# One-core attention and MoE kernel: attention visits split in two, a longer list of warm-up matmuls, unit 0's last rows by quadrants, and a new instruction order

## Chip, cores and metric

The kernel runs on one core of one Trainium2 chip. The metric is the device time in microseconds of one execution, the median of several runs. One further execution was taken under the hardware profiler, and all rows below come from it.

## What is computed (reference, cut)

A linear attention with per-channel decay (batch 4, 8 heads, 768 tokens, head size 48) gives a 3072 x 384 matrix; a two-layer MLP (384 to 2048 to 384) with a piecewise quadratic gate follows.

```python
for t in range(S):                       # per batch and head; state is 48 x 48
    cur = einsum('bhd,bhe->bhde', u * kt, vt)
    y[:, :, t] = einsum('bhd,bhde->bhe', rt, state + cur)
    state = wt[..., None] * state + einsum('bhd,bhe->bhde', kt, vt)
x = y.transpose(0, 2, 1, 3).reshape(3072, 384)
h = x @ w_in
g = h where h >= 1, 0 where h <= -1, else (h + 1)**2 / 4
out = g @ w_out
```

## The kernel before

**Tiling.** The tokens are cut into 12 attention *units* of 256 tokens (u0 to u11), two to a *block* of 512 tokens (b0 to b5). The MLP runs block by block in *steps* over the 16 slices f of 128 hidden columns. The first 8 steps of each half of block 0 and the first 11 of each half of block 1 treat 256 tokens (half steps), the others 512 (whole steps); there are 115 steps, n0 to n114. Step n has on TensorE an IN (`product_in`, L1040, nine passes; for n0 to n7 `product_in_whole`, L1046, six passes in full fp32) and an OUT (`product_out`, L1070; for n0 to n7 `product_out_whole`, L1052). Between them ScalarE and VectorE form the gate (`g`, `gh`, `gl`, L819 to L825). An fp32 matmul appears in the trace as two passes, each with its own weight load.

**Attention on TensorE.** A unit visits TensorE several times between the products, with small matmuls (64 or 48 rows and columns) that occupy one quadrant of the array each. In order: AMONGu (`among` with u, units 0 to 3 only, 64 passes, L475), AMONG (`among` with k, 64 passes, L475), KTRANS (transposes of k, units 0 to 3, 4 passes per half, L515; from unit 4 on VectorE and small DMAs do this), UMAT (`umat`, 64 passes, L533), then CROSS and ALONG or, for late units, CORNERS, ALONG, CORNERS (all through `put`, L612, 128 passes). VectorE works between them: two scans per half unit (L434, L429), the products k*=y (L455) and r*=p (L505), masked copies out of PSUM (`picked`, L481), and the state chain (`chain`, L581 to L587) between UMAT and CROSS. r*=p overwrites what AMONGu reads, so it follows AMONGu on VectorE. AMONG needs both r*=p.

**Units 4 to 11 before.** `VISIT` gives each the step after which its attention is entered; `late` is true, and `first_visit` runs AMONG and UMAT as one TensorE operation, with a bank of the hidden product (`hp`) as fourth PSUM bank.

**Start.** `warm` (L311 to L312) writes zeros into all eight PSUM banks with one fp32 matmul of 128 x 128 x 512 each, 16 passes in all; it is first on TensorE, and AMONGu of unit 0 follows it. Unit 0 ends with SPREAD (`spread`, L718): its last rows are moved between the other rows with three 128 x 128 matmuls per group g, two groups, 12 passes; they are copied out before that (last_f, L723). x_all is then copied (L693) and IN n0 may start. LESS (`less`, L709) subtracts the high part of unit 0's x.

**Weights.** A weight slice is loaded by SP (`fetch`, L332, 768 KB), joined from two halves on VectorE (`join`, L336) and split into a high part on ScalarE (L358) and a low part by a subtraction on VectorE (L361).

**Order.** Every engine executes its own instructions in order. That order is `ORDER`, a list of operation numbers written out by hand; an operation's number is its place among the calls of `op()`. The costs in the `op()` calls order nothing while `ORDER` is given; they only place the zero matmuls that fill long gaps.

Of the kernel before, what the change touches and what calls it, by code (L numbers as in the profile page):

```python
# [28 lines left out]
HP = 64  # L29
# [6 lines left out]
NB = NT // WIDE  # L36
# [15 lines left out]
class Plan:  # L52
# [101 lines left out]
VISIT = {4: 37, 5: 46, 6: 56, 7: 63, 8: 71, 9: 78, 10: 87, 11: 94}  # L154
# [72 lines left out]
)  # L227


def attention_moe(tc, a):  # L230
# [149 lines left out]
    def attention(u, when, spare=None):  # L380
# [220 lines left out]
        if late:  # L601
            by.append(take())
# [538 lines left out]
```

## Time and profile before

| | us |
|---|---|
| median of 3 runs | 498.87 (498.66 to 499.46) |
| profiled execution | 497.06 |
| its span, first to last instruction | 495.2 |
| TensorE busy in the span | 485.5 (98%) |
| VectorE busy | 343.8 (69%) |
| ScalarE busy | 289.6 (58%) |
| GpSimd busy | 56.7 (11%) |

TensorE's busy time counts passes from start to modelled end, and passes overlap, so the rate of a stretch is better read from the distance between starts. VectorE's share is an average over a dense first quarter and a light rest.

### The profile page before, as it was taken

How to read it: one execution, taken by the hardware profiler on the slowest of the kernel's cores; microseconds unless marked ns; L12 is line 12 of the kernel's file. 1: busy time of each engine (PE TensorE's matmuls, PEld its weight loads, DVE VectorE, ACT ScalarE, POOL GpSimd, SP SyncE). 2: the span in 40 equal slices, each digit the busy share in tenths (PEclk: the TensorE clock that was granted, in tenths of full speed). 3: DMA queues.
4: the chain of work that ended last, by engine and by line, in shares of the span. 5: the costliest groups of instructions: out<-in, count | busy, mean ns of one | idle time of the engine just before them, and what ended most of it. 6: DMA issues, size and time to landing. Idle time of an engine off the chain costs nothing.

```text
span 495.2 us, 12991 instructions
## 1 busy us (share of the span) xinstructions
PE 485.5 (98%) x5402; PEld 404.8 (82%) x5402; DVE 343.8 (69%) x597; ACT 289.6 (58%) x592; POOL 56.7 (11%) x60
## 2 busy tenths in 40 slices
PE   9799999999999999999999999999999999999997
PEld 4688998778999988888888888888888888888886
DVE  6899999998758768659679679469556745332333
ACT  3799889866656536746736646346626625552551
POOL 2332121300110101110110330020001000000000
PEclk9899999999999999999999999999999999999999
DMA  8995736225544344345245454225221110200001
GB/s 316 406 374 169 256 115 217 88 60 158 166 111 149 66 133 159 103 113 161 38 131 175 108 139 150 48 79 154 43 66 44 29 33 16 66 1 1 1 0 66
DMA packets 58749, 58.29 MB, mean 118 GB/s; under 512 B 38016, under 2 KB 47424, under 8 KB 58688
## 3 DMA queue, kind: packets, MB, share of 16 engines
q1 hardware_dynamic: 58256, 56.78, 37.4%
q8 instruction: 43, 0.70, 0.6%
q10 hardware_dynamic: 432, 0.66, 0.4%
q14 instruction: 18, 0.15, 0.1%
HBM read 46.34 MB, written 4.72 MB: 103 GB/s over the span
## 4 chain that ended last, share of the span: by engine, by line
PE 89%; DVE 5%; ACT 2%; issue 2%; DMA 1%; POOL 0%; DVEq 0%; SPq 0%; POOLq 0%
PE h L1040 37%; PE acc L1070 36%; PE bank L612 4%; PE bank L475 2%; PE bank L533 2%; PE acc L1052 2%; PE bank L1070 1%; PE h L1046 1%; PE bank L312 1%; DMA rk<-in_rk 1%; DVE r L481 1%; DVE wt L361 1%; PE acc L612 1%; DVE gl L825 1%; DVE rk L505 1%
## 5 line engine op out<-in xcount | busy, mean ns | idle before, releaser
L1040 PE MATMUL h<-x,wt 128*128 128x512 f32 (+1 forms) x963 | 207.4, 365 | 0.5 <-DVE g L821 0.4
L1040 PEld LDWEIGHTS h<-x,wt 128*128 128x128 f32 x963 | 162.5, 188 | 32.0 <-DVE g L821 0.9
L1070 PE MATMUL acc<-gh,wt 128*128 128x512 f32 (+1 forms) x642 | 146.4, 359 | 0.0
L821 DVE SCALAR_TENSOR_TENSOR g<-g,h 128x512 f32<-128x512 f32 (+1 forms) x115 | 67.8, 593 | 95.6 <-ACT g L820 95.1
L819 ACT ACTIVATE g<-h 128x512 f32<-128x512 f32 (+1 forms) x115 | 60.4, 526 | 119.2 <-PE h L1040 117.4
L1070 PEld LDWEIGHTS acc<-gh,wt 128*128 128x128 f32 x642 | 107.9, 188 | 18.7
L825 DVE TENSOR_TENSOR gl<-g,gh 128x512 fp32r<-128x512 f32 (+1 forms) x107 | 68.9, 648 | 17.1 <-ACT gh L824 10.6
L1070 PE MATMUL acc<-gl,wt 128*128 128x512 f32 (+1 forms) x321 | 80.7, 358 | 0.0
L824 ACT CAST gh<-g 128x512 fp32r<-128x512 f32 (+1 forms) x107 | 59.1, 556 | 33.1 <-DVE g L821 22.3
L820 ACT ACTIVATE g<-g 128x512 f32<-128x512 f32 (+1 forms) x115 | 64.4, 561 | 3.1
L1070 PEld LDWEIGHTS acc<-gl,wt 128*128 128x128 f32 x321 | 55.2, 188 | 9.1
L434 DVE TENSOR_TENSOR_SCAN p<-wq,seeds 128x514 f32<-128x514 f32 x24 | 30.8, 1283 | 10.8 <-DMA kt<-p 7.2
L501 POOL TENSOR_TENSOR r<-cst,d 128x512 f32<-128x512 f32 x16 | 17.0, 1084 | 152.2 <-DVE d L498 71.8
L429 DVE TENSOR_TENSOR_SCAN y<-wq,seeds 128x514 f32<-128x514 f32 x24 | 30.1, 1254 | 0.8
L346 POOL CAST rr<-fl 128x768 f16<-128x768 f32 x16 | 21.3, 1332 | 71.2 <-ACT fl L342 32.7
L493 POOL TENSOR_TENSOR nk<-nk 128x768 f32<-128x768 f32 x8 | 15.3, 1913 | 96.8 <-DMA nk<-in_nk 87.9
L455 DVE TENSOR_TENSOR rk<-rk,y 128x512 f32<-128x512 f32 x24 | 17.1, 712 | 2.6 <-DMA rk<-in_rk 2.1
L505 DVE TENSOR_TENSOR rk<-rk,p 128x512 f32<-128x512 f32 x24 | 17.0, 717 | 0.7 <-DMA rk<-in_rk 0.4
L345 ACT ACTIVATE rr<-wraw 128x768 uint16<-128x768 uint32 x16 | 17.3, 1079 | 0.2 <-DVE wa L336 0.2
L342 ACT ACTIVATE fl<-wraw 128x768 f32<-128x768 f32 x16 | 14.7, 917 | 1.0 <-DVE wt L361 1.0
L481 DVE COPY_PREDICATED r<-cst,bank 128x512 f32<-128x512 int32 x20 | 14.5, 729 | 1.0 <-PE h L475 0.5
L612 PEld LDWEIGHTS bank<-rk,st 48*48 48x48 f32 x656 | 11.4, 119 | 4.2 <-issue 1.8
(116 smaller groups left out, 447.8 us busy)
## 6 DMA issues: line engine op xcount, KB each, us to landing
rk<-in_rk SPq DMA_DIRECT2D x24, 512.0 KB, 5.3
wraw<-in_wbits SPq DMA_DIRECT2D x16, 768.0 KB, 6.9
wq<-in_w SPq DMA_DIRECT2D x24, 258.5 KB, 3.0
nk<-in_nk SPq DMA_DIRECT2D x8, 768.0 KB, 4.9
vn<-in_v SPq DMA_DIRECT2D x11, 384.0 KB, 4.4
kt<-p SPq DMA_DIRECT2D x128, 32.0 KB, 1.9
fl<-in_w SPq DMA_DIRECT2D x12, 257.0 KB, 3.4
x<-last SPq DMA_DIRECT2D x66, 32.0 KB, 2.0
```

The costliest lines, as they stand in the source:

```text
L346: op("POOL", SIGN, due, [("fl", k)], ["rr_high"], lambda: G.tensor_copy(rr.bitcast(F16).rearrange("p (c two) -> p c two", two=2)[:, :, 1], s))
L429: V.tensor_tensor_scan(out=y_[:, ::-1], data0=w[:, SEG:0:-1], data1=sv[:, ::-1], initial=0.0, op0=ALU.mult, op1=ALU.add)
L434: V.tensor_tensor_scan(out=pv[:, q].rearrange("p n c -> p (n c)"), data0=w[:, 0:SEG], data1=sv, initial=0.0, op0=ALU.mult, op1=ALU.add,)
L505: op("DVE", 0.69, due, [("p", q)], [("r", slot[q])], lambda q=q: V.tensor_tensor(out=parts(q, 0), in0=parts(q, 0), in1=pv[:, q, :, 0:UT], ...
L612: PE.matmul(out=bank[by[g]][HP * half : HP * half + wide, lo : lo + C], start=first, stop=False, skip_group_check=True, **kw)
L819: op("ACT", c, due, [("b", 6 + hk)], [("g", gk)], lambda: nc.scalar.activation(gs, hs, AF.Relu, scale=0.5, bias=0.5))
L820: op("ACT", c, due, (), [("g", gk)], lambda: nc.scalar.activation(gs, gs, AF.Square))
L821: op("DVE", 0.13 + 0.53 * k, due, [("b", 6 + hk)], [("g", gk)], lambda: nc.vector.scalar_tensor_tensor(out=gs, in0=gs, scalar=1.0, in1=hs, ...
L824: op("ACT", c, due, [("g", gk)], [("gh", gk)], lambda: nc.scalar.copy(ghs, gs))
L825: op("DVE", 0.15 + 0.5 * k, due, [("g", gk), ("gh", gk)], [("gl", gk)], lambda: nc.vector.tensor_tensor(out=gls, in0=gs, in1=ghs.bitcast(F ...
L1040: nc.tensor.matmul(hp, lhsT=wx[f][:, cs], rhs=xt[:, j, :], start=n == 0, stop=n == 8)
L1070: nc.tensor.matmul(o, lhsT=wx[f][:, 384 + j * 128 : 512 + j * 128], rhs=gt[:, 0 : cs.stop - cs.start] if gt.shape[1] < cs.stop else gt[:, cs],
```

## The change

Five edits:

1. `VISIT` is empty. Units 4 to 11 are entered with their block (at its predecessor's first step), so `late` is false and AMONG and UMAT are two operations again, on the three rotating PSUM banks. The form CORNERS, ALONG, CORNERS is kept for them by the new `side`.
2. `warm` begins with 39 fp32 matmuls of 64 x 64 x 64 (78 passes) in one quadrant; the first three banks are then cleared by two matmuls each in diagonal quadrants (12 passes), the other five as before (10 passes).
3. `spread` uses two 64 x 64 matmuls in diagonal quadrants for each 128 x 128 one (24 passes), as a quadrant operation.
4. The cost of `first_visit` in the list is changed; with no late unit it is not used.
5. `ORDER` is new (1791 numbers for 1783). In it, among much else, unit 0's loads stand in the order w1, perm, rk1, w0, rk0, cst, v (before: w1, w0, perm, rk1, rk0, v, cst), three weight loads stand ahead of unit 1's loads (before: between them), IN n0 stands ahead of LESS, and between the two visits that were one there are two to nine products.

```diff
-VISIT = {4: 37, 5: 46, 6: 56, 7: 63, 8: 71, 9: 78, 10: 87, 11: 94}
+VISIT = {}
+SMALL = 39
+SIDE = 4
...
     def warm():
-        for b in bank:
+        for _ in range(SMALL):
+            PE.matmul(bank[0][0:64, 0:64], lhsT=zero[0:64, 0:64], rhs=zero[0:64, 0:64], start=True, stop=True)
+        for b in bank[0:3]:
+            for i in (slice(0, 64), slice(64, 128)):
+                PE.matmul(b[i], lhsT=zero[i, 0:64], rhs=zero[i].unsqueeze(1).broadcast_to([64, 4, 128]), start=True, stop=True)
+        for b in bank[3:8]:
             PE.matmul(b, lhsT=zero, rhs=zero.unsqueeze(1).broadcast_to([128, 4, 128]), start=True, stop=True)
...
-        late = spare is not None
+        late, side = spare is not None, u >= SIDE
...
-            op("PE", 1.64, due, [("k", slot[0]), ("k", slot[1]), *both, *turns, *vk], [("b", i) for i in (*ba, *bu)], first_visit, apart=True)
+            op("PE", 1.89, due, [("k", slot[0]), ("k", slot[1]), *both, *turns, *vk], [("b", i) for i in (*ba, *bu)], first_visit, apart=True)
...
         by = [take(), take()]
-        if late:
+        if side:
             by.append(take())
...
-                PE.matmul(yv[:, j], lhsT=perm[:, 128 * j : 128 * j + 128], start=False, stop=True, skip_group_check=True,
-                          rhs=last_f.rearrange("p (c g t) -> p c g t", c=2, g=2)[:, :, g, :])
+                for h in range(2):
+                    i, lo = slice(HP * h, HP * h + HP), 128 * j + HP * h
+                    PE.matmul(yv[i, j], lhsT=perm[i, lo : lo + HP], start=False, stop=True, skip_group_check=True,
+                              rhs=last_f.rearrange("p (c g t) -> p c g t", c=2, g=2)[i, :, g, :])
...
-                op("PE", 0.35, due, [("last_f", g), "perm", "nk", ("g", 2)], [("b", by[g])], lambda g=g: spread(g), fresh=False)
+                op("PE", 0.3, due, [("last_f", g), "perm", "nk", ("g", 2)], [("b", by[g])], lambda g=g: spread(g), fresh=False, apart=True)
...
-        if n == WHOLE:
-            for u in (2, 3):
-                attention(u, step_of(u))
+        if n == WHOLE or b and f == 0 and cs.start == 0 and b + 1 < NB:
+            for u in (2 * b + 2, 2 * b + 3):
+                if u not in VISIT:
+                    attention(u, step_of(u))
```

## Rows read from the trace of the kernel before

**Rows 1.** Stretches of 5 us: us, busy time of each engine, clock, DMA.
```profile
15.00:20.00 5.00, 2.74 (x112) 2.50 (x112) 4.18 (x8) 2.56 (x3) 1.21 (x2) 0.92 1.03 398
20.00:25.00 5.00, 4.56 (x29) 3.90 (x24) 4.22 (x8) 3.77 (x8) 2.06 (x1) 0.74 1.01 406
...
95.00:100.00 5.00, 4.47 (x20) 3.25 (x19) 5.00 (x5) 3.58 (x6) 3.44 (x2) 1.00 0.06 21
```

**Rows 2.** Timeline of the start: start us, us, engine, line, operation, [idle before <-releaser].
```profile
1.07 5.05 PE L312 MATMUL bank<-zero 128*128 128x512 f32 x6 [1.07 <-POOL zero L296]
...
2.94 0.34 PEld L312 LDWEIGHTS bank<-zero 128*128 128x128 f32 x1 [0.52 <-issue]
...
3.80 0.34 PEld L312 LDWEIGHTS bank<-zero 128*128 128x128 f32 x1 [0.52 <-issue]
...
5.96 2.74 PE L312 MATMUL acc<-zero 128*128 128x512 f32 x6
...
8.53 1.88 PE L312 MATMUL h<-zero 128*128 128x512 f32 x4
...
8.67 0.91 ACT L445 ACTIVATE nk<-rk,wq 128x256 f32<-128x256 f32 x2 [0.55 <-DMA rk<-in_rk]
...
10.34 1.02 PEld L475 LDWEIGHTS acc<-rk,nk 64*64 64x64 f32 x64 [0.76 <-ACT nk L445]
...
11.11 1.29 DVE L505 TENSOR_TENSOR rk<-rk,p 128x512 f32<-128x512 f32 x2 [0.22 <-PE acc L475]
11.43 0.85 PEld L515 LDWEIGHTS bank<-cst,rk 128*128 128x128 f32 x8
11.44 1.09 PE L515 MATMUL bank<-cst,rk 128*128 128x128 f32 x8
```

**Rows 3.** Stretches of 0.5 us around unit 0's ALONG, columns as in rows 1.
```profile
18.50:19.00 0.50, 0.50 (x44) 0.50 (x41) 0.47 (x3) 0.00 (x0) 0.00 (x0) 1.00 1.06 394
...
19.50:20.00 0.50, 0.50 (x26) 0.50 (x20) 0.00 (x0) 0.00 (x0) 0.00 (x0) 0.50 1.07 421
```

**Rows 4.** Chain that ended last, in order of time: start us, us, what.
```profile
16.06 1.44 issue
...
133.37 1.07 PE h L1040 x9
...
151.80 1.94 PE bank L612 x128
...
200.57 4.20 PE h L1040 x18
...
366.10 1.26 PE bank L533 x63
```

**Rows 5.** TensorE's costliest groups, one of them: busy us, mean ns, idle before.
```profile
L718 PE MATMUL acc<-g,nk 128*128 128x128 f32 x12 | 2.5, 391 | 0.3 <-ACT g L723 0.3
```

**Rows 6.** Timeline of TensorE around unit 2's AMONG and UMAT.
```profile
57.97 1.16 PE L475 MATMUL bank<-rk 64*64 64x64 f32 x64
59.06 1.33 PE L1040 MATMUL h<-x,wt 128*128 128x256 f32 x9
60.23 0.60 PE L515 MATMUL bank<-cst,rk 128*128 128x128 f32 x4
...
65.02 0.94 PE L533 MATMUL bank<-vn,kt 64*48 64x48 f32 x64
65.89 1.33 PE L1040 MATMUL h<-x,wt 128*128 128x256 f32 x9
```

**Rows 7.** Timeline of TensorE, one of the eight merged visits.
```profile
286.85 0.27 PE L475 MATMUL bank<-rk 64*64 64x64 f32 x1
...
287.83 1.12 PE L533 MATMUL bank<-vn,kt 64*48 64x48 f32 x64
288.88 1.66 PE L1070 MATMUL acc<-gh,wt 128*128 128x512 f32 x6
```

**Rows 8.** Timeline of TensorE around unit 3's first transposes.
```profile
99.95 0.66 PE L515 MATMUL bank<-cst,rk 128*128 128x128 f32 x4 [0.53 <-DVE r L481]
```

More of the change, by code (lines that the diff above doesn't have):

```diff
@@ L635, in along @@
         def along(heads=(0, 1)):
-            if not late and 0 in heads:
+            if not side and 0 in heads:
                 crossed(0)
@@ L656, in attention @@
         y512 = y_[:, 0:512].rearrange("p (a c t) -> p a c t", a=4, t=C)
-        if late:
+        if side:
             third_bank = bank[by[2]].rearrange("p (a c t) -> p a c t", a=4, t=C)
```

122 rows, old and new, of the table ORDER are left out of this document.

## The prediction, as put on record before the result was known

> **What bounds the kernel now.** I read the chain that ended last first, then TensorE's timeline, then the 5 us stretches. On the chain a whole product is 4.20/2 = 2.10 us for nine passes and a half product 1.07 us [rows 4]; the products stand on it back to back almost from the first to the last. So a microsecond by which TensorE's first product comes later is a microsecond at the end, unless TensorE waits somewhere later and the lateness is used up in that wait. There is such a wait, and VectorE makes it. VectorE is busy 5.00 of 5.00 us in 95 to 100, while TensorE has 4.47 [rows 1], and unit 3's transposes wait 0.53 us for a masked copy [rows 8].
>
> How much TensorE waits in all I take from a stretch without other shapes: unit 2's UMAT starts at 65.02 [rows 6], unit 4's CORNERS at 151.80 [rows 4], 86.78 us. Between them stand 16 whole products (33.6), 36 half ones (38.4) and the visits: two UMAT and two AMONG-like visits at about 1.05 and 1.28 with their turns [rows 6], four half transposes at 0.5 [rows 2], two CROSS with ALONG at 2.3 (the 1.94 of the 128 passes in rows 4, and its drain), one merged visit at 2.3. That is 84.5 us, so **2.3 us are waits for VectorE**.
>
> Before the first product the chain is one of dependencies: warm-up, AMONGu, r*=p, AMONG, UMAT, state chain, CROSS, ALONG, SPREAD, x_all, IN n0. VectorE idles there for lack of inputs: 0.82 us in 15 to 20 and 0.78 us in 20 to 25, 1.6 us in all [rows 1]. Two things are behind it. TensorE stands for 1.44 us in CROSS with nothing to wait for that the profile shows [rows 4], and the granted clock falls from 1.00 to 0.50 in the second half of ALONG [rows 3], after TensorE was busy for only 2.74 of 5 us [rows 1]. SPREAD then runs at 391 ns a pass [rows 5].
>
> **The change part by part.** *Warm-up.* A pass of 512 columns starts 0.86 us after the one before at the low level of the clock (1.2 GHz; loads at 2.94 and 3.80) and 0.43 us after it at the high one (2.4 GHz; six passes from 5.96 to 8.53) [rows 2]; the rate of the passes shows the level here. It changes near 5.5 us. Sixteen passes end at 5.96 + 10 x 0.43 = 10.25, and AMONGu starts at 10.34 [rows 2]. Its data were there earlier: the last scaled copy ends at 8.67 + 0.91 = 9.58 [rows 2]. So the warm-up sets the start, and any lengthening counts in full. A tiny pass has 64 columns, an eighth: 0.107 us low, 0.054 high. From 1.07 to 5.5 that is 41 passes, the other 37 take 2.0, up to 7.5. Twelve diagonal passes go two abreast: 6 x 0.43 = 2.6, or 3.0 if the pairs overlap only in part as they are ordered. Ten full passes take 4.3. The sum ends at 14.4 to 14.8, against 10.25: **+4.4 us** for AMONGu. Behind it wait r*=p (11.11 before, at once after AMONGu [rows 2]) and with it all of VectorE's queue, which has nothing to do between about 11 and 15 us, and ScalarE's copies of the transposes.
>
> The lower bound of this term comes from the nearest rows at the other end. In sets of four quadrants 44 passes touch half a microsecond at the high level and 26 at the low one [rows 3], 0.011 and 0.019 us each. If a lone tiny pass cost only its share of a set, 78 would take 0.9 to 1.5 us, more of the later passes would run at the low level, and the warm-up would end near 10.8: +0.5. I take 0.107, because one quadrant streams its own 64 columns whatever the other three do. The upper bound: if tiny passes in a quarter of the array don't raise the clock, they last 78 x 0.107 = 8.3 us to 9.4, some full passes follow at 0.86, and the end is near 17.5: +7.3.
>
> *What the start gives back.* With AMONGu 4.4 us late VectorE has a full queue, and its 1.6 us of idleness go but for 0.1: **-1.5**. The 1.44 us and the half-speed clock are inside this term. TensorE is denser there, so I expect the clock to stay up until ALONG; it may fall while TensorE waits for x_all at about 24 to 27 us, which would slow the first products: **+0.3** taken, 0 to 1.3 as bounds.
>
> *SPREAD.* 24 passes, two abreast, stream as long as 12; only the turn between quadrant and full passes moves behind it: 0. It is covered by VectorE, which in the new order has a scan ahead of last_f and another ahead of x_all; without that cover it saves some 0.1.
>
> *New order at the start.* Decoding the lists by counting operations: up to the state chain of unit 1 VectorE has 37 instructions instead of 38 (one weight subtraction less, about 0.97 us by the r*=p row scaled from 512 to 768 columns, 1.29/2 x 1.5 [rows 2]); TensorE has one product of the full kind less ahead of unit 1's CROSS (six passes of 256 columns, 6 x 0.21 = 1.3). Both engines are about as tight there as before: **+0.3**.
>
> *New order later.* At OUT n16 the same TensorE work stands ahead in both lists, but 99 VectorE instructions instead of 102; missing are a scan, a k*=y and two subtractions, and one weight join has come in, 2 us and more. At unit 3's CROSS TensorE has two more half products ahead and VectorE about the same. So VectorE's lead grows by 2 us or more where TensorE now waits, and the **-2.3** of waits go. Bounds: 0 and -2.3; there is no more to take.
>
> *Visits apart.* The merged visit takes 288.88 - 286.85 = 2.03 us [rows 7], and some are longer: one has 1.26 us in its UMAT on the chain [rows 4]; the eight average 2.13. Alone, AMONG takes 1.09 and UMAT 0.87 [rows 6], 1.96 together, and a second turn costs 0.1 ahead and 0.1 after (1.17 for the half product after AMONG [rows 6], against 1.07 [rows 4]). 2.16 against 2.03 to 2.13, for eight units: **+0.1**, 0 to +1.0. SP's and POOL's queues keep their instructions; only their order changes, and the unit loads keep the slack of a whole block.
>
> *A rule against the change.* The two transposes of unit 0 use all rows of the array in each pass, and eight loads and eight passes took 1.09 us together [rows 2]: loads and passes overlap although they share rows, and 0.107 stands. The Trainium skill says otherwise (TensorE: Matmul & The Clock Gate, Part 3: Packing small matmuls): a weight load overlaps running matmuls only when its row group is another one, and all tiny passes share theirs. The trace disagrees; by that rule the sum would be that of rival D, by the rows it is the one below.
>
> *Loads.* On SP's queue w0 of unit 0 now has perm and rk1 (704 KB) ahead of it, 1.8 us at about 400 GB/s [rows 1]; unit 1's first loads have two weights more ahead, 1.57 MB or 3.9 us. Both are hidden by the later AMONGu: 0. Without that cover the first would cost up to 1.8 us.
>
> Sum: 4.4 - 1.5 + 0.3 + 0.3 - 2.3 + 0.1 = **+1.3 us**. The profiled execution took 497.06 (span 495.2 and 1.9 around it), which makes 498.4. The median of the three runs lies 1.8 above the profiled one; I carry the difference over: 498.87 + 1.3 = 500.2.
>
> **Rivals.** *A: a tiny pass is cheap, and the kernel gets faster.* The place is the first 15 us. With the lower bound (+0.5) the sum is -2.6: 496.3. With the high-level price of 0.054 from the first pass on the warm-up ends near 12.4, the term is 2.2 and the sum -0.9: 498.0. It decides below 0.054 us a tiny pass. For it: no row shows a lone quadrant's pass at the low level. Against it: full passes scale with the clock, and so did ALONG's [rows 3].
>
> *B: the delay is absorbed.* If VectorE's queue before x_all is shorter than TensorE's dependencies, the 1.44 us and the slow SPREAD come back as well, 1.2 more than I credit: sum 0.1, 499.0. Against it: two scans and two joins stand before x_all in VectorE's list.
>
> *C: the clock stays low through the tiny passes.* +7.3 in place of 4.4: sum +4.2, 503.1. For it: the clock fell in ALONG, whose passes are quadrant passes too [rows 3]. Against it: TensorE would be without a gap.
>
> *D: the loads don't overlap in one quadrant.* Each tiny pass then pays load and stream; the loads of the transposes are 0.85 us for eight with overlap [rows 2], so 0.11 at least is added to each of 78, +8: 508. This is what the rule of the Trainium skill named above (TensorE: Matmul & The Clock Gate, Part 3: Packing small matmuls) comes to.
>
> *E: the new order brings a wait of its own*, for instance in units 5 and 7, where one product alone, 2.1 us, stands between UMAT and CORNERS for the three additions of the state chain. The merged form had a single product there in unit 5, with two masked copies in it as well, and TensorE didn't wait. I put it inside my range, at up to +1.
>
> **How the numbers follow.** My forecast (500.2, own range 499.2 to 501.8) gets 0.45; A 0.27; B 0.18; C 0.06; D 0.02; the rest is open. 0.2% of 498.87 is 1.0 us, about what a measurement of this kernel can tell from no change. Faster by over 0.2%: most of A, 0.27. Slower: nearly all of my forecast, C and D, 0.49. Within: B and the edges, 0.24. The range reaches down to A's lower end and up short of C: 496.1 to 502.6.
>
> **What would show it.** In the changed profile the last pass of the warm-up and the first of AMONGu should stand at 14 to 15 us (10.34 before); before 12.5 means A, after 17 means C or D. IN n0 should come 3 to 4 us later than unit 0's LESS did; VectorE should have one gap from about 11 to 15 us and nearly none from there to 25. From 75 to 105 us TensorE should wait less than before, and 5 us stretches there should show it full. AMONG and UMAT of units 4 to 11 should take about 1.1 and 0.9 us. I am wrong if TensorE's first product comes no later than before, or if TensorE's waits move to other places in the new order.

## The result, and the profile after

The changed kernel takes 504.80 us (median of 4 runs, 504.18 to 505.07), against 498.76 (498.56 to 499.46) before on the same chip: 1.0122 times, 95% interval 1.0097 to 1.0148. That is 6.0 us slower, outside my range (496.1 to 502.6), and 4.6 us above the predicted 500.2. The direction was the one with the largest chance; the size is that of rival C and something more. The profiled executions are 504.18 and 497.06 us, spans 502.4 and 495.2: +7.2. The one before lies 1.7 below its median, the one after 0.6, so the terms read from the two traces add up to 7.2 and not to 6.0.

In the code of the changed kernel the lines have moved: the tiny passes are L314, the diagonal ones L317, the full ones L319, AMONGu and AMONG L482, r\*=p L512, UMAT L540, CROSS and ALONG L619, SPREAD L727, IN n0 L1056, IN L1050, OUT L1080.

TensorE's timeline of the start, after (start us, us, engine, line, operation, idle before):

```profile
1.07 8.47 PE L314 MATMUL bank<-zero 64*64 64x64 f32 x77 [1.07 <-POOL zero L298]
...
9.45 3.82 PE L317 MATMUL bank<-zero 64*64 64x512 f32 x11
13.20 2.84 PE L319 MATMUL acc<-zero 128*128 128x512 f32 x6
15.88 1.88 PE L319 MATMUL h<-zero 128*128 128x512 f32 x4
17.69 1.16 PE L482 MATMUL acc<-rk,nk 64*64 64x64 f32 x64
```

All 78 tiny passes go by at 0.107 us each, the price at the low level (1.2 GHz), from 1.07 to 9.4. Six diagonal pairs last from 9.24 to 13.20; two and a half of them go at 0.86 a pair, so the rate doubles only between 11 and 12 us, where it did so near 5.5 before. As in the prediction, the level is read from the distance between passes: the column of the granted clock has 1.00 even where they go at the low rate (us, busy us of PE, PEld, DVE, ACT, POOL, granted clock, DMA share, GB/s):

```profile
5.00:9.00 4.00, 4.00 (x40) 4.00 (x39) 3.43 (x7) 1.47 (x5) 0.00 (x0) 1.00 1.01 383
```

AMONGu starts at 17.69 instead of 10.34 [rows 2]: +7.35, where I had put 4.4.

VectorE's and TensorE's timelines further on, after:

```profile
18.45 1.29 DVE L512 TENSOR_TENSOR rk<-rk,p 128x512 f32<-128x512 f32 x2 [7.62 <-PE acc L482]
...
30.04 1.32 PE L1056 MATMUL h<-vn,wa 128*128 128x256 f32 x5 [0.16 <-DVE seeds L440]
```

VectorE has nothing to do for 7.62 us, then is busy for 11.10 of the 11.44 us up to x_all's end (29.89), and IN n0 starts at 30.04. Before, TensorE began at 23.21 with LESS what then runs on without a gap:

```profile
23.21 0.55 PE L709 MATMUL acc<-x,minus 128*128 128x128 f32 x3
23.81 1.56 PE L1046 MATMUL h<-vn,wa 128*128 128x256 f32 x6
```

So **6.83 us** of the 7.35 are still there, and 0.5 are given back. From r\*=p to TensorE's first work VectorE is idle for 0.39 of 11.59 us, before for 1.65 of 12.10, so 1.26 of its idleness went. But it is busy for 11.20 us there, before for 10.45. Its copy of x_all (0.53 us), beside which TensorE ran LESS before, now stands ahead of IN n0, and one addition of the state chain took three times as long (before, then after):

```profile
18.95 0.36 DVE L587 TENSOR_TENSOR st<-sm,ptot 128x192 f32<-128x192 f32 x1
```

```profile
24.73 1.05 DVE L594 TENSOR_TENSOR st<-sm,ptot 128x192 f32<-128x192 f32 x1
```

Why that addition is slower, no run shows.

The 5 us stretches in which TensorE waited before are 95 to 100 [rows 1, 8] and the next one. This one before, then both after (columns as above):

```profile
100.00:105.00 5.00, 4.63 (x80) 3.56 (x81) 5.00 (x9) 3.62 (x8) 0.00 (x0) 1.00 0.36 87
```

```profile
95.00:100.00 5.00, 5.00 (x55) 4.13 (x47) 4.82 (x8) 4.59 (x9) 1.27 (x2) 1.00 0.64 204
100.00:105.00 5.00, 5.00 (x23) 4.03 (x22) 4.88 (x8) 4.96 (x10) 3.22 (x2) 1.00 0.03 7
```

The waits for VectorE near 100 us are gone. Others of the same size have come in: TensorE's waits from 31 us on (us in total, times, longest), before and then after:

```profile
PE bank L515 <- DVE r L481: 0.5, 1, 0.5
PE h L1040 <- DVE g L821: 0.4, 1, 0.4
```

```profile
PE bank L482 <- DVE r L488: 0.5, 1, 0.5
PE h L1056 <- DVE g L830: 0.4, 1, 0.4
PE bank L619 <- issue: 0.2, 1, 0.2
```

The two for VectorE stand at 99.95 and 100.98 before, at 37.38 and 35.07 after, where unit 1's visits had a single wait of 0.66 us before (27.60).

TensorE's last pass, before and then after:

```profile
491.80 0.28 PE L1070 MATMUL bank<-gl,wt 128*128 128x256 f32 x1
```

```profile
497.28 0.28 PE L1080 MATMUL bank<-gl,wt 128*128 128x256 f32 x1
```

That is **+5.48**, 1.35 less than at IN n0. Idle time of over 0.1 us between passes, from LESS or IN n0 on, adds up to 1.9 us before and 1.3 after, so only 0.6 of the 1.35 can be read as waits that went.

The visits apart, after:

```profile
297.82 0.94 PE L540 MATMUL bank<-vn,kt 64*48 64x48 f32 x64
298.69 1.66 PE L1050 MATMUL h<-x,wt 128*128 128x512 f32 x6
...
328.31 1.16 PE L482 MATMUL bank<-rk 64*64 64x64 f32 x64
329.40 0.96 PE L1050 MATMUL h<-x,wt 128*128 128x512 f32 x3
```

From start to start UMAT takes 0.87 us and AMONG 1.09, as forecast.

What is left is behind TensorE's last pass. From its start to the span's end it was 495.2 - 491.80 = 3.4 us and is 502.4 - 497.28 = 5.1. The last two DMA issues, before and then after (queue, KB, median us from issue to landing):

```profile
out_y<-g SPq DMA_DIRECT2D x1, 128.0 KB, 1.7
out_y<-y ACTq DMA_DIRECT2D x1, 128.0 KB, 1.7
```

```profile
out_y<-g SPq DMA_DIRECT2D x1, 128.0 KB, 2.8
out_y<-y ACTq DMA_DIRECT2D x1, 128.0 KB, 3.4
```

The last output takes 1.7 us longer from its issue to its landing, a term that my sum didn't have. So the 7.2 us of the span are 6.83 (start) - 1.35 (waits and visits) + 1.7 (end).

### The profile page after: what moved, and what is told of

Read it like the earlier page. It is cut to its first block, busy times and chain, and to the rows that moved or that the text cites. A ratio compares the mean times of both kernels' runs of the same rounds, so it can differ in the third digit from the quotient of the medians.

```text
span 502.4 us, 13203 instructions
## 1 busy us (share of the span) xinstructions
PE 491.6 (98%) x5500; PEld 409.8 (82%) x5500; DVE 347.3 (69%) x597; ACT 290.6 (58%) x592; POOL 55.8 (11%) x60
## 4 chain that ended last, share of the span: by engine, by line
PE 95%; DVE 2%; DMA 1%; ACT 0%; issue 0%; SPq 0%; POOL 0%; POOLq 0%; DVEq 0%
PE h L1050 39%; PE acc L1080 38%; PE bank L619 4%; PE bank L482 3%; PE acc L1062 2%; PE bank L540 2%; PE bank L314 2%; PE h L1056 1%; DMA wraw<-in_wbits 1%; PE bank L1080 1%; PE bank L317 1%; PE acc L319 1%; PE bank L522 1%; DVE r L488 1%; DVE rk L512 1%; PE h L319 0%
## 5 line engine op out<-in xcount | busy, mean ns | idle before, releaser
L1050 PE MATMUL h<-x,wt 128*128 128x512 f32 (+1 forms) x963 | 208.0, 366 | 0.0
L1050 PEld LDWEIGHTS h<-x,wt 128*128 128x128 f32 x963 | 161.5, 188 | 30.3
L1080 PE MATMUL acc<-gh,wt 128*128 128x512 f32 (+1 forms) x642 | 146.4, 359 | 0.0
L1080 PEld LDWEIGHTS acc<-gh,wt 128*128 128x128 f32 x642 | 108.4, 188 | 19.3
L1080 PE MATMUL acc<-gl,wt 128*128 128x512 f32 (+1 forms) x321 | 80.7, 358 | 0.0
L834 DVE TENSOR_TENSOR gl<-g,gh 128x512 fp32r<-128x512 f32 (+1 forms) x107 | 67.3, 639 | 19.1 <-ACT gh L833 12.5
L1080 PEld LDWEIGHTS acc<-gl,wt 128*128 128x128 f32 x321 | 55.2, 188 | 9.1
L488 DVE COPY_PREDICATED r<-cst,bank 128x512 f32<-128x512 int32 x28 | 20.1, 734 | 5.8 <-PE bank L482 4.8
L512 DVE TENSOR_TENSOR rk<-rk,p 128x512 f32<-128x512 f32 x24 | 16.8, 705 | 7.8 <-PE acc L482 7.6
L619 PEld LDWEIGHTS bank<-rk,st 48*48 48x48 f32 x656 | 11.5, 119 | 4.4 <-issue 2.6
L619 PE MATMUL bank<-rk,st 48*48 48x64 f32 x656 | 14.5, 220 | 0.5 <-issue 0.2
```

The lines of the kernel that those rows point to most:

```text
L488: V.copy_predicated(out=r_[h].rearrange("p a b c -> p (a b) c"), mask=mask.unsqueeze(1).broadcast_to([128, 8, C]), data=bank[of].rearrange ...
L512: op("DVE", 0.69, due, [("p", q)], [("r", slot[q])], lambda q=q: V.tensor_tensor(out=parts(q, 0), in0=parts(q, 0), in1=pv[:, q, :, 0:UT], ...
L619: PE.matmul(out=bank[by[g]][HP * half : HP * half + wide, lo : lo + C], start=first, stop=False, skip_group_check=True, **kw)
L834: op("DVE", 0.15 + 0.5 * k, due, [("g", gk), ("gh", gk)], [("gl", gk)], lambda: nc.vector.tensor_tensor(out=gls, in0=gs, in1=ghs.bitcast(F ...
L1050: nc.tensor.matmul(hp, lhsT=wx[f][:, cs], rhs=xt[:, j, :], start=n == 0, stop=n == 8)
L1080: nc.tensor.matmul(o, lhsT=wx[f][:, 384 + j * 128 : 512 + j * 128], rhs=gt[:, 0 : cs.stop - cs.start] if gt.shape[1] < cs.stop else gt[:, cs],
```

## The experiments

Theory 1: one quadrant alone leaves the clock low, and AMONGu's lateness goes through to the end. Rival: the order or the visits carry the loss. The ratios are against the kernel before in runs on the same chip; its medians there lay between 498.07 and 499.19 us.

**The warm-up by itself, in both kernels.** In the changed kernel the old warm-up comes back:

```diff
-        for _ in range(SMALL): ...
-        for b in bank[0:3]: ...
-        for b in bank[3:8]:
+        for b in bank:
             PE.matmul(b, lhsT=zero, rhs=zero.unsqueeze(1).broadcast_to([128, 4, 128]), start=True, stop=True)
```

> The changed kernel with the old warm-up (eight full fp32 matmuls, 16 passes). Theory (the clock stays low through the tiny passes and that lateness goes to the end): AMONGu starts at 10.3 us instead of 17.69, IN n0 at 23.5 to 24.5 instead of 30.04, and the time is 504.8 less 5.5 to 7.3 us, 497.5 to 499.3; if the later landing of the last output (3.4 instead of 1.7 us) hangs on where TensorE's last instructions are fetched, it may move by another 1.7 us, down to 495.8. Rival (the new order and the visits apart carry the loss; the warm-up only fills time in which VectorE would have been the limit): IN n0 no earlier than 26, time 501 to 503.

Measured: 501.50 us, 1.0051 (1.0026 to 1.0076). AMONGu starts at 10.01, 7.7 us earlier, but IN n0 only 4.2 earlier, at 25.83, and the time falls by 3.3. The theory misses: 497.5 to 499.3 and an IN n0 at 23.5 to 24.5 were expected. The time is in the rival's range (501 to 503), and IN n0 is just short of the 26 that it asked for. The warm-up is over half of the loss, and an early AMONGu doesn't give back all that its delay cost. Two rows of TensorE's timeline say why:

```profile
18.00 0.27 PE L614 MATMUL acc<-rk,g 48*64 48x64 f32 x1 [1.09 <-issue]
...
24.50 0.44 PE L722 MATMUL acc<-g,nk 64*64 64x128 f32 x4 [0.99 <-issue]
```

TensorE stands twice (in CROSS and in SPREAD) with nothing to wait for that the profile shows, like the 1.44 us of before [rows 4]. In the start of the changed kernel there is no such row of over 0.3 us.

The kernel before with the new `warm` and nothing else:

> The kernel before with the new warm-up and nothing else (78 tiny passes, 12 diagonal, 10 full). Theory: AMONGu at 17.7 us, later by 7.3; the idle time of VectorE at the start (1.6 us) is given back in part, so unit 0's LESS comes 5.5 to 7.3 us later, and VectorE's later lead uses up at most 2.3 us of it: 498.8 plus 3.5 to 6.5 us, 502.3 to 505.3. Rival (the loss belongs to the new order): within 2 us of the kernel before, 498.8 to 500.8.

Measured: 503.75 us, 1.009 (1.0068 to 1.0113), in the theory's range. The first pass of AMONGu, and TensorE's two waits for VectorE that stood near 100 us before (here at 106.17 and 107.20):

```profile
18.25 1.16 PE L482 MATMUL acc<-rk,nk 64*64 64x64 f32 x64
```

```profile
PE bank L522 <- DVE r L488: 0.5, 1, 0.5
PE h L1047 <- DVE g L828: 0.4, 1, 0.4
```

Unit 1's visits are 6.2 us later than before, the last pass 5.85 later. The two waits are still there, so it is the new order that took them away, not the lateness. The last output lands in 1.9 us, so the end isn't the warm-up's doing.

**What raises the clock.** Three kernels change only the tiny passes of the changed kernel.

```diff
-        for _ in range(SMALL):
-            PE.matmul(bank[0][0:64, 0:64], lhsT=zero[0:64, 0:64], rhs=zero[0:64, 0:64], start=True, stop=True)
+        for _ in range(5):                       # long_in_one_quadrant
+            PE.matmul(bank[0][0:64], lhsT=zero[0:64, 0:64], rhs=zero[0:64].unsqueeze(1).broadcast_to([64, 4, 128]), ...)
+        for n in range(SMALL):                   # same_count_two_quadrants; 2 * SMALL in tiny_on_diagonal
+            i = slice(64 * (n % 2), 64 * (n % 2) + 64)
+            PE.matmul(bank[0][i, 0:64], lhsT=zero[i, 0:64], rhs=zero[i, 0:64], start=True, stop=True)
```

> The changed kernel in which the 39 tiny matmuls of 64 columns are replaced by 5 matmuls of 512 columns in the same quadrant (10 passes of 0.86 us at the low level, 8.6 us in all, where the tiny ones took 8.4). If it is the single quadrant that leaves the clock low, all ten passes take 0.86 us, the clock rises only some 4 us into the passes that follow, and AMONGu starts at 17.7 to 18.2 as in the changed kernel. If it is the shortness of the passes (each with its own weight load), the clock rises near 5.5 us as before, the rest of the ten take 0.43, and AMONGu starts at 12.8 to 14.5.

Measured: one time, 508.54 us. TensorE's timeline:

```profile
1.07 7.94 PE L314 MATMUL bank<-zero 64*64 64x512 f32 x9 [1.07 <-POOL zero L298]
...
8.87 3.75 PE L317 MATMUL bank<-zero 64*64 64x512 f32 x11
12.54 2.84 PE L319 MATMUL acc<-zero 128*128 128x512 f32 x6
15.22 1.88 PE L319 MATMUL h<-zero 128*128 128x512 f32 x4
17.03 0.38 PE L482 MATMUL acc<-rk,nk 64*64 64x64 f32 x9
```

All passes of 512 columns in the one quadrant take 0.85 us, and the rate rises only among the diagonal ones, near 10 us. AMONGu starts at 17.03, a little ahead of the 17.7 to 18.2 expected and far from the 12.8 to 14.5 of the other case. So it isn't the shortness of the passes. Nor is 0.85 merely what one quadrant costs at either level: the diagonal pairs behind start at that rate too. The time of this one execution says little, as TensorE stands for 3.05 us in UMAT.

> The changed kernel in which the tiny matmuls are 78 (156 passes), alternating between two diagonal quadrants, so that two run abreast for the same 8.4 us at the low level. If half of the array in tiny passes is enough to raise the clock, as the 12 diagonal passes of 512 columns seem to be, the clock rises near 5.5 us, the later tiny pairs take 0.054, and AMONGu starts at 14 to 15 us. If short passes never raise it, all 78 pairs take 0.107 and AMONGu starts at 17.7.

Measured: one time, 504.51 us. TensorE's timeline:

```profile
1.07 6.60 PE L315 MATMUL bank<-zero 64*64 64x64 f32 x156 [1.07 <-POOL zero L298]
7.51 2.74 PE L318 MATMUL bank<-zero 64*64 64x512 f32 x12
...
14.67 0.52 PE L483 MATMUL acc<-rk,nk 64*64 64x64 f32 x20
...
20.86 0.20 PE L541 MATMUL h<-g,kt 64*48 64x48 f32 x1 [2.49 <-issue]
```

In two quadrants the pairs go at 0.11 us up to about 5.2 us and at 0.06 from there: the clock rises about when it did under full passes. AMONGu starts 3.0 us earlier than in the changed kernel. Nothing of it arrives, since TensorE stands for 2.49 us in UMAT; that is taken up below.

> The changed kernel with one difference: its 39 tiny matmuls go in turn to two diagonal quadrants instead of all to one; the number of TensorE instructions is the same. Theory (one quadrant leaves the clock low, two raise it): the 39 pairs take some 4.2 us, the clock rises near 5 us, AMONGu starts at 12 to 12.5 us instead of 17.69, IN n0 at 24.5 to 26 instead of 30.04, and the time is 4 to 5.5 us below the 504.8 of the changed kernel, 499.3 to 500.8; the fetches of instructions lie at the same instructions as in the changed kernel, so no new stall is expected in the dense visits. Rival (the lateness comes from the number of short instructions): AMONGu at 16 or later, time above 503.

Measured: 501.51 us, 1.005 (1.0023 to 1.0077). AMONGu is at 12.11, as expected; the pairs' rate doubles near 4.4 us. The time is 3.3 us below the changed kernel's, short of the 4 to 5.5 expected, and IN n0 is at 28.92 instead of 24.5 to 26. TensorE's timeline shows stalls where I expected none:

```profile
16.23 0.27 PE L483 MATMUL h<-rk 64*64 64x64 f32 x1 [0.98 <-issue]
...
22.48 1.99 PE L620 MATMUL acc<-r,g 64*64 64x64 f32 x64 [2.23 <-issue]
```

and stretches of 2 us show what follows one (columns as above):

```profile
20.00:22.00 2.00, 0.26 (x12) 0.12 (x5) 1.93 (x5) 1.80 (x2) 1.04 (x1) 0.87 1.00 371
22.00:24.00 2.00, 1.52 (x57) 1.52 (x60) 0.73 (x1) 0.00 (x0) 0.00 (x0) 0.50 0.91 311
...
26.00:28.00 2.00, 2.00 (x19) 1.67 (x16) 1.95 (x4) 0.23 (x1) 1.88 (x1) 0.50 0.58 230
```

TensorE has 0.26 of 2 us, and then ALONG and SPREAD run at a granted clock of 0.50. The moment at which the rate doubles in the warm-up isn't fixed, and each kernel has one profile. Under full passes it was at about 4.5 to 5.5 us in five kernels. Where the warm-up begins on two diagonal quadrants it was at 4.4 to 7.3 us in eight, four of which have the same 106 passes and show 5.9 to 7.3. Where it begins on one, it was at 10 to 13 us in three.

**The stalls without a releaser.** Theory 2: they are waits for instructions. Near each stands a fetch of 16 KB on DMA queue q8, of which a run has 43 to 45. Which engine's instructions a fetch brings isn't in the profile; that these are TensorE's is inferred. The counts speak for it: 43 fetches go with 10,894 to 10,923 recorded instructions of TensorE (passes, weight loads and the sequencer's own), 44 with 10,955 to 11,103, 45 with 11,247, about 250 a fetch, while the other engines have some 2,100 in all. Read from the DMA packets and TensorE's timeline:

```
kernel                      fetch begins  stalled pass starts  between  in
before                      14.94         17.51                2.57     CROSS
after_old_warm              15.57         18.00                2.43     CROSS
                            21.95         24.50                2.55     SPREAD
long_in_one_quadrant        21.47         23.98                2.51     UMAT
tiny_on_diagonal            18.48         20.86                2.38     UMAT
same_count_two_quadrants    13.84         16.23                2.39     AMONG
                            19.98         22.48                2.50     ALONG
```

In the changed kernel the fetches begin at 21.11 and 25.30. TensorE stands anyway from 21.7 to 23.10 for the state chain and from 25.5 to 27.29 for last_f, so only 0.3 us of the two show, in CROSS. If theory 2 holds, more instructions ahead move the stall without any change to the visit. That is tried by cutting warm-up matmuls of 512 columns into sixteen of 64 columns on two diagonal quadrants, which takes the same time:

```diff
-        for b in bank:
+        for b in bank[0:2]:                      # bank[0:3] in the cuts of three
+            for c in range(0, 512, 64):
+                for i in (slice(0, 64), slice(64, 128)):
+                    PE.matmul(b[i, c : c + 64], lhsT=zero[i, 0:64], rhs=zero[i, 0:64], start=True, stop=True)
+        for b in bank[2:]:
             PE.matmul(b, lhsT=zero, rhs=zero.unsqueeze(1).broadcast_to([128, 4, 128]), start=True, stop=True)
```

> The kernel before, whose first two warm-up matmuls of 512 columns are cut into 32 matmuls of 64 columns on the two diagonal quadrants, which take the same 3.4 us at the low level and add about 120 TensorE instructions ahead of everything else. Theory (TensorE's instructions come in fetches of 16 KB; it stands until some 2.5 us after such a fetch begins when the fetch falls into a dense stretch of small passes, and the number of instructions ahead says where): AMONGu stays at 10.3, but the stall of 1.44 us in CROSS is gone from there and stalls of 1 to 3 us appear at other dense stretches, or none; the time moves by up to 2.5 us either way. Rival (the stall belongs to CROSS itself, whatever stands ahead): 1.44 us in CROSS again, the time within 0.5 us of the kernel before.

Measured: 500.50 us, 1.0023 (0.9997 to 1.0049). AMONGu starts at 10.32. TensorE's timeline, and the queue row of the DMA view from 13.7 to 14.9 us (packets, MB, share):

```profile
16.30 0.24 PE L537 MATMUL h<-g,kt 64*48 64x48 f32 x2 [2.37 <-issue]
...
22.58 1.34 PE L616 MATMUL acc<-r,g 64*64 64x64 f32 x40 [1.39 <-issue]
```

```profile
q8 instruction: 1, 0.02, 5.3%
```

The stall has left CROSS; there is one in UMAT and one in ALONG, 2.52 and 2.66 us after the fetches at 13.78 and 19.92. With nothing added ahead it stays in CROSS: 1.58 and 1.64 us in the two kernels further down that keep the warm-up of before (`before_check_early`, `before_spread_quarters`).

> The changed kernel with the old warm-up cut in the same way (about 120 TensorE instructions more ahead, the same 3.4 us). Theory (fetches of instructions): the stalls of 1.09 us in CROSS, 0.99 us in SPREAD and 1.6 us at two later visits move or go; the time moves by 1 to 3 us against the 501.5 without the cut. Rival: the stalls stay at the same instructions and the time within 0.5 us.

Measured: 501.78 us, 1.0058 (1.0032 to 1.0083). The stalls moved:

```profile
15.67 0.24 PE L539 MATMUL h<-g,kt 64*48 64x48 f32 x2 [1.85 <-issue]
...
22.10 1.34 PE L618 MATMUL acc<-r,g 64*64 64x64 f32 x40 [1.87 <-issue]
```

They end 2.47 and 2.62 us after fetches begin (13.20, 19.48), and the two at later visits are gone. The theory's 1 to 3 us miss: the median is within 0.3 us of the uncut one, as the rival had it; here the new stalls cost what the old ones had.

> The kernel before with its first three warm-up matmuls cut into 48 (about 180 TensorE instructions more ahead, AMONGu at 10.3 us as before). By the theory of the fetches the stall moves again: against the cut of two, where it stood 2.37 us in UMAT and 1.39 in ALONG, it comes some 60 instructions earlier, in AMONG or at UMAT's start and in CROSS; the time lies between 498 and 501. Rival: 2.4 us in UMAT as with the cut of two, time 500.5.

Measured: 499.51 us, 1.0015 (0.999 to 1.0039). The stall is in CROSS (1.68 us, ending at 19.39, 2.49 after the fetch at 16.90). AMONGu is at 10.98 instead of 10.3, since the rate doubled later, near 6.8 us. Of the two stalls expected one came, the one in CROSS. The other, in AMONG or at UMAT's start, didn't: the fetch ahead of it began at 8.51, under the warm-up. Two stalls further on, 1.03 us at 148.19 and 1.23 at 298.34, weren't expected.

So the tie to the fetch stands: in all 16 kernels there are 27 such rows of over 0.3 us, and each ends 2.3 to 2.7 us after a fetch begins. It doesn't hang on the load of the DMA engines: 19 of them come at 370 to 420 GB/s, eight (one in UMAT of `long_in_one_quadrant`, seven after 140 us) at 10 to 70, with the same distance. That the number of instructions ahead says where a stall falls is borne out in part only. It moved with that number in three kernels, but `same_count_two_quadrants` has as many as the changed kernel, and its fetches fall at other instructions. No run takes the fetches away, so that TensorE waits for them remains inferred.

**The end.** Theory 3. Near its end the kernel tests whether the inputs lie in the range that its fast way is written for (the final check): a matmul of one column gives a number, VectorE makes a flag of it, and a branch on TensorE, VectorE and GpSimd behind everything skips a general way. In the new order this matmul and the flag stand three passes earlier, so the fetches behind the branch come while the last output is still in flight. Both ways:

```diff
 # check_late: the changed kernel with the old warm-up
-    "1739 1740 1744 1741 1746 1745 1789 1742 1747 1790 1743 1748 1750 1749 1751 "
+    "1739 1740 1744 1741 1746 1745 1742 1789 1747 1743 1748 1790 1750 1749 1751 "
 # before_check_early: the kernel before
-    ... 1738 1737 1734 1781 1739 1735 1740 1782 1742 1741 1743 "
+    ... 1738 1737 1781 1734 1739 1782 1735 1740 1742 1741 1743 "
```

> The changed kernel with the old warm-up, and the final check's matmul and its flag moved behind the third but last group of passes, where the kernel before has them (three passes later). Theory (the new order makes the flag three passes earlier, the code behind the verdict's branch is then fetched while the last output is still in flight, and that output lands in 3.4 us instead of 1.7): the last output lands in 1.7 to 1.9 us, the time from TensorE's end to the span's end falls from 4.8 to 3.2 us, and the time is 1.3 to 1.7 us below the 501.5 of the same kernel with the early check: about 500. Rival (the landing hangs on where the instruction count puts the last fetch): landing stays at 3.4 and the time at 501.5.

> The kernel before with the final check's matmul and its flag three passes earlier, where the new order has them. Theory (early flag, early fetch, late last output): landing of the last output 3.4 us instead of 1.7, time up by 1.3 to 1.7 us. Rival (where the instruction count puts the last fetch): no change within 0.5 us.

Measured: 500.06 us, 1.0021 (0.9995 to 1.0047), by the ratios 1.5 us less than with the check early; and 500.99 us, 1.0066 (1.0035 to 1.0096), by the medians 2.1 us more than before and by the ratio 3.3, both above the 1.3 to 1.7 expected. The last DMA issue of the one with the check late, then of the one with it early:

```profile
out_y<-y ACTq DMA_DIRECT2D x1, 128.0 KB, 1.9
```

```profile
out_y<-y ACTq DMA_DIRECT2D x1, 128.0 KB, 3.4
```

The landing goes with the place of the check, and not with the instruction count: it is 1.7 to 1.9 us in all nine kernels profiled with the late check, 3.4 to 3.7 in the seven with the early one. In span, from TensorE's end, the early check costs the kernel before 1.7 us (4.9 against 3.1). What the second kernel has above that arises elsewhere: its profiled execution was already 1.9 us late at unit 4, with no edit ahead of that. In the packets, the three fetches (two on q14, one on q8, 32 KB together) begin at 493.89 to 494.22 us before, when the output's last packet ends (493.94), and at 498.66 to 499.45 after, where the last packets end at 501.00; of the last dozen some take 0.13 us instead of at most 0.05. How 32 KB hold the output up for that long, no run shows.

**The best of both.** The changed kernel with the check late and three warm-up matmuls cut, which brings its instruction count near that of the changed kernel:

> The changed kernel with the check late and the old warm-up's first three matmuls cut into 48 on diagonal quadrants (106 warm-up passes where the changed kernel has 100 and the old warm-up 16), meant as the best of both: early AMONGu (10.3 us), early check, and nearly the changed kernel's instruction count, by which the fetches fall into waits that TensorE has anyway. Theory: no issue stall over 0.5 us in the dense visits, IN n0 at 24 to 25, last output landing in 1.7 to 1.9 us, time 497 to 498.5 against 498.9 before. Rival (the fetches meet TensorE at another moment, as it is 7 us earlier against loads and VectorE): stalls of 1 to 2.5 us again and the time at 499.5 to 501.

Measured: 498.25 us, 0.9988 (0.9964 to 1.0013), in the theory's range, but not for its reason. AMONGu starts at 11.16 instead of 10.3, as the rate doubled only near 7 us, and IN n0 at 25.27 instead of 24 to 25. The landing is 1.8, as expected; one stall remains, ending 2.52 us after the fetch at 17.25:

```profile
19.77 0.21 PE L618 MATMUL acc<-rk,g 48*64 48x64 f32 x1 [1.68 <-issue]
```

The time is that of the kernel before: with the warm-up and the end mended, the new order, the visits apart and SPREAD in quadrants together are worth nothing that can be measured (by the interval 1.8 us less to 0.6 more). Two things in its start were tried for the rest: `IDLE` raised so that no zero matmul fills the gap ahead of IN n0, and then also operation 19 (w0 of unit 0) moved ahead of 25 and 18 in `ORDER`.

> The kernel with the late check and three cut warm-up matmuls (498.25 us), without the zero matmul that fills the gap ahead of IN n0 (2 passes, 24.31 to 25.27 us there, while x_all is ready at 24.91). If the filler only holds up IN n0, that starts at 24.9 to 25.0 and the time falls by 0.3 us, to about 498. If it keeps the clock up, IN n0 starts at 24.9 but its passes take twice as long for some microseconds (six passes of 256 columns at 0.43 instead of 0.21), and the time rises by 1 to 2 us.

> The kernel without the filler, and with unit 0's w0 loaded ahead of perm and rk1, as in the kernel before. In the version it comes from, VectorE's third scan waits 1.85 us for that load and r*=p starts at 12.12, where AMONGu alone would allow 11.9. Theory: the wait goes, r*=p starts 0.2 to 0.4 us earlier and the time falls by as much, within 0.5 us of the one without filler. Rival (the later perm or rk1 is late next, or TensorE's fetches meet another moment): no gain, or 1 to 2 us worse with an issue stall in UMAT or CROSS.

Measured: 498.15 us, 0.9999 (0.9977 to 1.0021), and 498.46 us, 1.0007 (0.9981 to 1.0033). Neither shows a difference. Without the filler the first kernel's six passes of IN n0 take 2.4 us instead of 1.1, at a granted clock of 0.50, and start at 25.60; the second's go at 1.00 and start at 24.84. So what the filler does for the clock isn't settled. With w0 early VectorE's wait for it is gone, but r\*=p starts at 12.01 instead of 12.12, since AMONGu is late next.

Last, SPREAD in quadrants in the kernel before (the diff of the change, that part alone):

> The kernel before with SPREAD alone done in quadrants (24 passes for 12). By my forecast that is worth nothing: SPREAD takes 24 x 0.1 us as before, since two passes run abreast, IN n0 at 23.8, the time 498 to 499. Rival (the half passes don't overlap): SPREAD 2.5 us longer and the time 500.5 to 501.5; and as some 24 TensorE instructions more stand ahead of all that follows, a fetch can fall elsewhere and move it by 1 us either way.

Measured: 498.87 us, 1.0018 (0.9992 to 1.0044): nothing that can be told from zero, though 2 us more aren't excluded. In its profile a stall of 0.90 us in SPREAD ends 2.41 after a fetch begins, and IN n0 is at 25.09 instead of the 23.8 expected.

That the visits are apart was not tried by itself, since a list of operations for that would be another order.

## Why the prediction was right or wrong

- **Warm-up, +4.4 forecast, +7.35 measured.** This is the step that failed: "From 1.07 to 5.5 that is 41 passes, the other 37 take 2.0". It took the time at which the clock rose under full passes for the tiny ones too. They run in one quadrant, and there the clock stays at its lower level for as long as they last; in two quadrants as many of them raised it near 4.4 us, twice as many near 5.2. The upper bound (17.5, +7.3) was right to 0.2 us, and I gave it 0.06. What I set against it, that TensorE would have no gap, is what the runs refute. The row that I had for it, the half clock in ALONG, pointed the right way by luck: in the changed kernel ALONG, with less idle time ahead of it, runs at 1.00, so quadrant passes alone don't explain that fall.
- The Trainium skill (TensorE: Matmul & The Clock Gate, Part 1: The HAM clock gate) calls the warm-up a budget of time, not a number of matmuls, and has everything after it run at the high level. This trace disagrees: 8.4 us of back-to-back passes in one quadrant stayed at 0.107 us.
- **Price of a tiny pass, 0.107 at the low level: right.** 78 took 8.4 us. Rival A (cheap) and D (load and stream one after the other, 0.11 more each) are both out.
- **The start gives back 1.5, less 0.3 and 0.3: forecast -0.9, measured -0.5.** VectorE's queue was full from r\*=p on: 1.26 us of its idleness went, near the 1.5. The clock was 1.00 throughout, so the 0.3 put down for its fall wasn't needed. What took it back is 0.75 us more work on VectorE ahead of TensorE's first work, where I had put 0.3. The 1.44 us in CROSS did go. But I let it go with VectorE's idleness; by theory 2 it is a wait for instructions, and it went because the fetches came to lie in waits.
- **Later waits -2.3 and visits +0.1: forecast -2.2, measured -1.35.** The mechanism was right in part: the two waits near 100 us go with the new order, and remain in the old one when only the warm-up is new. But two of the same size stand at 35 and 37 us instead, the sign that I had named for being wrong. The 2.3 was a remainder of counted shapes, and only 0.53 of it is idle time in a row that I showed [rows 1, 8], and 0.9 in all up to 105 us. The terms as written, with four half transposes, even add up to 85.6 and leave 1.2; the trace has two in that stretch, with which 84.6 and 2.2 come out. The visits by their own mean are 8 x 0.03, +0.2. How the rest divides between smaller waits and second turns isn't settled.
- **The end: 0 forecast (not in the sum), +1.7 measured.** The change was read as an order of loads, visits and VectorE's queue; that the last branch's flag had moved by three passes is in the new `ORDER`, and I gave it no term. Two runs show it, one each way.
- **SPREAD 0: right** as far as it was measured, which leaves up to 2 us open. **Loads 0: right** in the changed kernel, where the late AMONGu covers them; with an early AMONGu the third scan waited 1.3 to 2.8 us for w0, as the price without cover said (up to 1.8) or above it.
- Rival E (a wait of the new order's own in units 5 and 7) doesn't appear; the new order's own waits stand at unit 1's visits, at 35 and 37 us.

The misses add up: 2.95 + 0.4 + 0.85 + 1.7 = 5.9, which is 7.2 - 1.3.

## What to carry to other kernels

Before a filler or a warm-up is priced by the time at which the clock rose, ask what part of the array its passes occupy, and price the case that the clock never rises in it. A TensorE stall that no semaphore explains, in or behind a stretch of many small passes, may be a wait for a fetch of instructions. Its place can then move when an edit far away changes the number of instructions ahead, and the time with it by one to two microseconds either way; a run with the same work in more instructions, and the distance from the last fetch, tell it. Read the end of a new order as carefully as its start: in these kernels the place of the last branch's flag decided whether fetches came while the last output was in flight.

## What the runs showed of the hardware

- Passes in one of four quadrants, of 64 or 512 columns and without a gap, left TensorE at 1.2 GHz for as long as they ran, 7 to 8 us, in three kernels. Where pairs on two diagonal quadrants came first it rose to 2.4 GHz at 4.4 to 7.3 us, in eight, and under full passes at 4.5 to 5.5, in five. All this is read from the distance of passes.
- TensorE resumed 2.3 to 2.7 us after a 16 KB fetch of instructions began, in all twenty stalls without a releaser of the first 25 us, in fourteen kernels, and in seven later ones; at 370 to 420 GB/s of DMA traffic as at 10 to 70.
- The last output of 128 KB took 3.4 us to land instead of 1.7 when the fetches behind the final branch (two on q14, one on q8) came before its packets were through.
